# A pad of 224 bytes and one of 192: DMA-transposed tiles moved onto 256-byte boundaries

## Chip, cores and metric

The kernel runs on one core of a Trainium2 chip. The metric is device time in microseconds (us) of one execution of the whole program; lower is better. The profile is of one execution, and its span runs from the first to the last instruction.

## What is computed

The forward pass and all gradients of one block: a layer norm, multi-head attention (32 heads of 16 channels, sequence 2048, width 512) and a gated MLP (hidden width 1792) that multiplies the attention's output. Cut to what matters:

```python
def fwd(A_x, wqkv, wo, w1, b1, w2, b2):          # x: [1, 2048, 512]
    xn = layernorm(A_x)
    q, k, v = split_heads(xn @ wqkv)             # 32 heads, 16 channels each
    p = softmax(q @ k^T * 16 ** -0.5)            # [32, 2048, 2048]
    s = merge_heads(p @ v) @ wo
    h = gelu(layernorm(xn) @ w1 + b1)
    g = silu(h @ w2 + b2)
    return A_x + s * g
# outputs: fwd(...) and the gradients of all seven inputs for a given grad_out, all bf16
```

## The kernel before

**Stages.** `phase_pre` (to about 276 us) does the layer norms, the projections and the MLP forward, and writes per-head-pair operands to DRAM (`NAT_s`, `NATQq_s`, `NATQd_s`). `attention_core` (276 to 2524 us) does the attention forward and backward, with the instruction order as the code writes it. `phase3` (the rest) does the remaining gradients. Instructions of the two outer stages are ordered by the tile framework.

**The attention stage.** It goes over 16 pairs of heads and 4 chunks of 512 queries, 64 blocks of 16 steps; a step `g` takes one block of 128 keys. In a step:

- PE makes the scores `s` (line 648) and, for both heads, `d` (line 662, dP minus its row term); ACT writes `et` = exp(`s`) (line 676); DVE writes `gts` = `d` x `et` (line 697).
- PE adds `et` and `gts` into the sums `X` over keys (lines 729, 732, 744).
- For the gradients of K and V the same arrays are needed with queries on the partitions. `gts` is transposed by DMA into `gk` (line 710), one DMA for two steps: 128 partitions x 4096 bytes, 512 KB. Of `exp(s)`, the query blocks 1 and 3 are transposed by DMA from `et` into `ek` (line 716), two DMAs of 256 KB for four steps; blocks 0 and 2 are computed again by PE and ACT as `t` and `e` (lines 634, 684). PE adds `e`, `ek` and `gk` into `Z` (lines 807, 813) one block of 16 steps later, with a further lag of 3 steps.
- Once per pair of heads `NAT`, `NATQq`, `NATQd` are loaded, GpSimd lays them out in `KVPad` and `QDPad`, and two DMA transposes of 512 KB make `KVT` and `QDT` (lines 594, 602).

All DMA transposes, 512 + 512 + 16 + 16 = 1056, are issued on SyncE's queue in program order. Each is cut in tiles of 16 partitions x 128 elements, so that it reads rows of 128 x 2 = 256 bytes of one partition.

**Where tiles lie.** Tiles of a pool get consecutive addresses within a partition, each rounded up to 32 bytes. `persist` comes first and holds the two identities, `eps_t`, `rstd1` and `rstd2`, and everything after follows from its size. In `attention_core`, the pool `opnd` holds the operands (`KVT0` to `acc`), then come `et` (3 buffers), `gts` (4), `gk` (5), `ek` (10), `e` (5) and small tiles. Sizes from `acc` to `ek` are multiples of 256 bytes, so all buffers of one name have one offset from a 256-byte boundary; all blocks that a transpose reads within a tile start at multiples of 256 bytes from the tile's start.

Of the kernel before, what the change touches and what calls it, by code (L numbers as in the profile page):

```python
# [26 lines left out]
def make_identity(nc, ap):  # L27
    nc.gpsimd.memset(ap, 0.0)
    nc.gpsimd.affine_select(out=ap, in_=ap, compare_op=ALU.not_equal, fill=1.0, base=0,
                            pattern=[[-1, ap.shape[1]]], channel_multiplier=1)  # L30
# [512 lines left out]
def attention_core(ctx, tc, NAT_s, NATQ_s, Oall, dQall, dKVT_out, ident_f32, npairs=16, nqc=4):  # L543
# [4 lines left out]
    opnd = sb("opnd", 1)  # L548
# [27 lines left out]
    Lc = opnd.tile([128, 32], bf16, name="Lc")  # L576
    nc.gpsimd.memset(Lc[:], 0.0)
    nc.gpsimd.memset(Lc[:, 17:18], 1.0)
    acc = opnd.tile([64, S], f32, name="acc")

    def load_ops(p):
# [284 lines left out]
def full_kernel(ctx, tc, A_x, A_wqkv, A_wo, B_x, B_w1, B_b1, B_w2, B_b2, grad_out,  # L866
                out_0, out_1, out_2, out_3, out_4, out_5, out_6, out_7, dbg=None, phases=("01", "15", "att", "3")):
    nc = tc.nc
    dbg = dbg or {}
    k = K()  # L870
    persist = ctx.enter_context(tc.tile_pool(name="persist", bufs=1))
    k.ident_bf = persist.tile([128, 128], bf16, name="ident_bf")
    make_identity(nc, k.ident_bf[:])
    k.ident_f = persist.tile([128, 128], f32, name="ident_f")
    make_identity(nc, k.ident_f[:])
    k.eps_t = persist.tile([128, 1], f32, name="eps_t")
    nc.vector.memset(k.eps_t[:], EPS)
    k.rstd1 = persist.tile([128, NT], f32, name="rstd1")
    k.rstd2 = persist.tile([128, NT], f32, name="rstd2")

    def scratch(name, shape, dt=bf16):
        if name in dbg:
            return dbg[name]
        return tc.dram_tile(list(shape), dt, name=name)
    k.XN_s = scratch("XN_s", [S, D])
    k.Y_s = scratch("Y_s", [S, D])
    k.DSO_s = scratch("DSO_s", [S, D])
    k.H1T_s = scratch("H1T_s", [F, S])
    k.HG_s = scratch("HG_s", [S, F])
    k.DH1_s = scratch("DH1_s", [S, F])  # L890
    k.NAT_s = scratch("NAT_s", [NPAIR, 128, NT, 2 * NATW])
    k.NATQq_s = scratch("NATQq_s", [NPAIR, 128, NT, 34])
    k.NATQd_s = scratch("NATQd_s", [NPAIR, 128, NT, 32])
    k.GB_s = scratch("GB_s", [S, 2, D])
    k.dKVT_s = scratch("dKVT_s", [H * 32, S])

    if "01" in phases or "15" in phases:
        phase_pre(ctx, tc, k, A_x, A_wqkv, A_wo, B_w1, B_b1, B_w2, B_b2, grad_out, dbg)
    with ExitStack() as cO:
        pO = cO.enter_context(tc.tile_pool(name="persistO", bufs=1))  # L900
        k.Oall = pO.tile([128, NT, D], bf16, name="Oall")
        k.dQall = pO.tile([128, NT, D], bf16, name="dQall")
        if "att" in phases:
            with ExitStack() as cB:
                with tc.manual_schedule():
                    attention_core(cB, tc, k.NAT_s, (k.NATQq_s, k.NATQd_s), k.Oall, k.dQall, k.dKVT_s, k.ident_f)
        if "3" in phases:
            phase3(ctx, tc, k, A_x, A_wqkv, A_wo, B_w1, B_w2, grad_out, out_0, out_1, out_2, out_3, out_4, out_5, out_6, out_7, dbg)


@with_exitstack
def kernel(
    ctx: ExitStack,
    tc: tile.TileContext,
    A_x: bass.AP,
    A_wqkv: bass.AP,
    A_wo: bass.AP,
    B_x: bass.AP,
    B_w1: bass.AP,
    B_b1: bass.AP,  # L920
    B_w2: bass.AP,
    B_b2: bass.AP,
    grad_out: bass.AP,
    out_0: bass.AP,
    out_1: bass.AP,
    out_2: bass.AP,
    out_3: bass.AP,
    out_4: bass.AP,
    out_5: bass.AP,
    out_6: bass.AP,  # L930
    out_7: bass.AP,
):
    full_kernel(ctx, tc, A_x, A_wqkv, A_wo, B_x, B_w1, B_b1, B_w2, B_b2, grad_out,
                out_0, out_1, out_2, out_3, out_4, out_5, out_6, out_7)
# [30 lines left out]
```

## Time and profile before

| | |
|---|---|
| median of 2 runs | 3130.07 us (3129.59 to 3130.55) |
| the profiled execution | 3131.9 us, span 3130.1 us |
| busy in the span | PE 81%, DVE 65%, ACT 56%, GpSimd 20% |
| DMA traffic | 543.46 MB, mean 174 GB/s |
| DMA packets | 1831694, of which 1754785 under 512 bytes |
| SyncE's DMA queue (q1) | 486.70 MB, 85.3% of 16 engines' span |

A share of DMA is the time that the packets took, summed and divided by 16 engines and the time; packets of one engine can overlap, so that it can pass 1. PE, DVE, ACT, POOL and SP are the tensor, vector, scalar, GpSimd and sync engines; PEld is PE's weight load. In the views "x <- y" in a wait means that x waited until y ended; a row of a table by windows gives the stretch from:to in us, its length, the busy time of each engine, the granted PE clock, the DMA share and GB/s. For a DMA, "to landing" is from the start of its issue to its completion.

### The profile page before, as it was taken

What the parts mean: (1) busy time and instruction counts of PE and PEld (TensorE: products, weight loads), DVE (VectorE), ACT (ScalarE), POOL (GpSimd) and SP (SyncE); (2) the same over time, 40 slices, a digit from 0 to 9 for tenths busy, and PEclk for the clock granted to TensorE, in tenths of its full rate; (3) what the DMA queues carried; (4) which work ended last, traced back from release to release, by engine and by line L of the source; (5) the groups of instructions that cost most, each with busy time, mean ns of one, the idle gap of its engine ahead of it and who ended that gap; (6) DMA issues with size and microseconds to landing.
All of it is one profiled execution on the core that took longest, in us unless ns stands there. A gap on an engine that the chain in (4) does not pass through costs nothing. (4 is left out here: it accounts for less than half of the span.)

```text
span 3130.1 us, 49097 instructions
## 1 busy us (share of the span) xinstructions
PE 2535.6 (81%) x18944; PEld 791.9 (25%) x18944; DVE 2021.1 (65%) x3382; ACT 1755.6 (56%) x1973; POOL 621.0 (20%) x1023
## 2 busy tenths in 40 slices
PE   4786888888888888888888888888888876674977
PEld 2331222222222222222222222222222223332343
DVE  5764676766767676776767676676767745882034
ACT  2443676766667666666767666676767734441020
POOL 1333110111011110111011110101111024882015
PEclk8997898989989898888989899898989987887989
DMA  5435999999999999999999999999999983324531
GB/s 175 114 125 129 196 194 195 196 196 192 196 193 194 194 194 194 191 196 194 193 198 195 193 193 193 195 194 194 189 195 197 190 226 111 105 89 134 137 123 41
DMA packets 1831694, 543.46 MB, mean 174 GB/s; under 512 B 1754785, under 2 KB 1815586, under 8 KB 1831458
## 3 DMA queue, kind: packets, MB, share of 16 engines
q1 hardware_dynamic: 1758066, 486.70, 85.3%
q10 hardware_dynamic: 73392, 53.62, 5.6%
q8 instruction: 148, 2.42, 0.3%
q14 instruction: 88, 0.72, 0.1%
HBM read 65.41 MB, written 55.32 MB: 39 GB/s over the span
## 5 line engine op out<-in xcount | busy, mean ns | idle before, releaser
L697 DVE TENSOR_TENSOR gts<-d,et 128x512 bf16<-128x512 f32 x2048 | 1304.8, 683 | 630.8 <-DMA gk<-gts 274.2
L676 ACT ACTIVATE et<-s 128x1024 bf16<-128x1024 f32 x1024 | 1016.4, 1025 | 189.3 <-DMA ek<-et 82.3
L684 ACT ACTIVATE e<-t 128x1024 bf16<-128x1024 f32 x512 | 523.5, 1023 | 570.6 <-PE t L634 559.2
L662 PE MATMUL d<-QDT,KVT 32*128 32x512 bf16 x2048 | 617.6, 415 | 264.5 <-DVE gts L697 262.0
L648 PE MATMUL s<-QDT,KVT 32*128 32x512 bf16 x2048 | 430.8, 417 | 43.8 <-ACT et L676 29.1
L729 PE MATMUL X<-et,Lc 128*32 128x512 bf16 x2048 | 441.7, 428 | 12.5 <-DVE xs L750 12.3
L732 PE MATMUL X<-et,NAT 128*32 128x512 bf16 x2048 | 439.8, 427 | 0.0
L744 PE MATMUL X<-gts,NAT 128*17 128x512 bf16 x2048 | 437.6, 423 | 0.0
L813 PE MATMUL Z<-gk,W 128*32 128x512 bf16 x2048 | 436.6, 420 | 0.0
L777 POOL TENSOR_TENSOR W<-NATQd,rL 128x128 bf16<-128x128 bf16 x64 | 25.7, 401 | 1560.9 <-DVE rL L772 1560.9
L807 PE MATMUL Z<-e,W 128*32 128x512 bf16 x1024 | 221.6, 426 | 10.6 <-ACT e L684 7.3
L634 PE MATMUL t<-KVT,QDT 32*128 32x512 bf16 x1024 | 219.1, 425 | 0.0
L807 PE MATMUL Z<-ek,W 128*32 128x512 bf16 x1024 | 218.3, 423 | 0.0
L744 PEld LDWEIGHTS <-NAT 128*17 128x17 bf16 x2048 | 93.2, 88 | 488.9 <-issue 488.9
L648 PEld LDWEIGHTS <-KVT 32*128 32x128 bf16 x2048 | 102.4, 92 | 430.6 <-issue 430.0
L662 PEld LDWEIGHTS <-KVT 32*128 32x128 bf16 x2048 | 134.4, 92 | 253.7 <-issue 237.4
L729 PEld LDWEIGHTS <-Lc 128*32 128x32 bf16 x2048 | 105.3, 94 | 198.5 <-issue 198.5
L820 DVE TENSOR_TENSOR acc<-Z,acc 64x512 f32<-64x512 f32 x192 | 129.2, 673 | 21.1 <-PE Z L813 21.1
L807 PEld LDWEIGHTS <-W 128*32 128x32 bf16 x2048 | 121.5, 94 | 55.1 <-issue 48.3
L732 PEld LDWEIGHTS <-NAT 128*32 128x32 bf16 x2048 | 105.2, 100 | 63.0 <-issue 20.7
L813 PEld LDWEIGHTS <-W 128*32 128x32 bf16 x2048 | 106.8, 99 | 10.6 <-issue 4.8
L634 PEld LDWEIGHTS <-QDT 32*128 32x128 bf16 x1024 | 48.8, 92 | 234.7 <-issue 234.7
(200 smaller groups left out, 2611.6 us busy)
## 6 DMA issues: line engine op xcount, KB each, us to landing
gk<-gts SPq DMA_TRANSPOSE x512, 4.6
ek<-et SPq DMA_TRANSPOSE x512, 3.7
HG_s<-hg SPq DMA_DIRECT2D x16, 448.0 KB, 3.1
DH_s<-dh ACTq DMA_DIRECT2D x16, 448.0 KB, 2.5
NAT<-NAT_s SPq DMA_DIRECT2D x16, 264.0 KB, 3.0
GB_s<-gB ACTq DMA_DIRECT2D x16, 256.0 KB, 2.0
dKVT_s<-ob SPq DMA_DIRECT2D x16, 256.0 KB, 3.6
dhc<-DH_s ACTq DMA_DIRECT2D x2, 2048.0 KB, 13.9
```

What stands on the lines that cost most here:

```text
L634: nc.tensor.matmul(t[:, hj, :], lhsT=op["QDT"][r:r + 32, q0:q0 + 128], rhs=op["KVT"][r:r + 32, kc * 512:(kc + 1) * 512], start=True, stop= ...
L648: nc.tensor.matmul(s[:, hj, :], lhsT=op["KVT"][r:r + 32, kb * 128:(kb + 1) * 128], rhs=op["QDT"][r:r + 32, qc * 512:(qc + 1) * 512], start ...
L662: nc.tensor.matmul(d[:], lhsT=op["KVT"][r:r + 32, kb * 128:(kb + 1) * 128], rhs=op["QDT"][r:r + 32, qc * 512:(qc + 1) * 512], start=True, ...
L676: nc.scalar.activation(out=et[:, :, kb % 4, :, :].rearrange("k b h q -> k h b q"), in_=st_s.pop(g)[:].rearrange("k h (b q) -> k h b q", b= ...
L684: nc.scalar.activation(out=e[:], in_=st_t.pop(g)[:], func=ACT.Exp)
L697: nc.vector.tensor_tensor(out=gts[:, kb % 2, hj, :].rearrange("k (b q) -> k b q", b=4), in0=ds[hj][:].rearrange("k (b q) -> k b q", b=4), ...
L729: nc.tensor.matmul(X[64 + 32 * hj:96 + 32 * hj, :], lhsT=Lc[:], rhs=et[:, :, kb % 4, hj, :], start=(kb == 0), stop=False, skip_group_check ...
L732: nc.tensor.matmul(X[32 * hj:32 * hj + 32, :], lhsT=NATt[:, kb, hj, 1:33], rhs=et[:, :, kb % 4, hj, :], start=(kb == 0), stop=(kb == 15), ...
L744: nc.tensor.matmul(X[64 + 32 * hj:64 + 32 * hj + 17, :], lhsT=NATt[:, kb, hj, 0:17], rhs=gts[:, kb % 2, hj, :], start=False, stop=(kb == 1 ...
L807: nc.tensor.matmul(Z[32 * hj:32 * hj + 32, :], lhsT=blk[j]["W1"][:, qb, hj, :], rhs=ev[:, hj], start=(qb == 0), stop=False, tile_position= ...
L813: nc.tensor.matmul(Z[32 * hj:32 * hj + 32, :], lhsT=blk[j]["W2"][:, qb, hj, :], rhs=gv[:, :, :, hj, qb, :], start=False, stop=(qb == 3), t ...
L820: nc.vector.tensor_tensor(out=av, in0=Z[0:64, :], in1=av, op=ALU.add)
```

## The change

Two tiles are allocated that nothing reads or writes: 224 bytes at the end of `persist` and 192 bytes in `opnd` ahead of `acc`.

```diff
@@ attention_core
     Lc = opnd.tile([128, 32], bf16, name="Lc")
     nc.gpsimd.memset(Lc[:], 0.0)
     nc.gpsimd.memset(Lc[:, 17:18], 1.0)
+    opnd.tile([128, 192], mybir.dt.uint8, name="pad_to_256b")
     acc = opnd.tile([64, S], f32, name="acc")
@@ full_kernel
     k.rstd1 = persist.tile([128, NT], f32, name="rstd1")
     k.rstd2 = persist.tile([128, NT], f32, name="rstd2")
+    persist.tile([128, 224], mybir.dt.uint8, name="pad_to_256")
```

Every engine has the same instructions in the same order with the same waits as before; only addresses differ. The start of the tiles in a partition, as bytes past a 256-byte boundary:

| tile | role in a transpose | before | after |
|---|---|---|---|
| `KVPad`, `QDPad` | read | 32 | 0 |
| `gts` (4 buffers), `et` (3) | read | 96 | 0 |
| `gk` (5), `ek` (10) | written | 96 | 0 |
| `KVT0`, `QDT0` | written | 32 | 0 |
| `KVT1`, `QDT1` | written | 160 | 128 |
| `acc`, `e`, `xs`, `xt`, `W1`, `W2`, `ob` | none | 96 | 0 |
| `Oall`, `dQall`, `xnT`, `yT`, `dsoT`, and the weights loaded in `phase_pre` | none | 32 | 0 |
| `dmT`, `oT`, `dQT`, `xn_all`, `Rkv` and most of `phase3` | none | 64 | 32 |
| `xn`, `y`, `xt4`, `h1row`, `dso`, `hgc`, `dhc` | none | 192 | 160 |
| `h1T`, `xr`, `hg`, `gp`, `dh1` | none | 128 | 96 |

## Prediction

> **What bounds the kernel now.** First the page's totals and its 40 slices, to see which resource is full, and where.
>
> ```profile
> span 3130.1 us, 49097 instructions
> ...
> PE 2535.6 (81%) x18944; PEld 791.9 (25%) x18944; DVE 2021.1 (65%) x3382; ACT 1755.6 (56%) x1973; POOL 621.0 (20%) x1023
> ...
> PE   4786888888888888888888888888888876674977
> ...
> DMA  5435999999999999999999999999999983324531
> GB/s 175 114 125 129 196 194 195 196 196 192 196 193 194 194 194 194 191 196 194 193 198 195 193 193 193 195 194 194 189 195 197 190 226 111 105 89 134 137 123 41
> ...
> q1 hardware_dynamic: 1758066, 486.70, 85.3%
> ```
>
> From the fifth slice to the 32nd the DMA digit is 9, while PE stands at 8. No compute engine is full there. The next view cuts the span at the first transpose (276 us) and after the last one (2524 us).
>
> ```profile
> core 0: us, PE busy (x) PEld busy (x) DVE busy (x) ACT busy (x) POOL busy (x), PEclk, DMA share, GB/s
> 0.00:276.00 276.00, 182.07 (x912) 85.67 (x912) 164.89 (x340) 101.97 (x177) 91.94 (x98) 0.91 0.44 135
> 276.00:2524.00 2248.00, 1925.88 (x15582) 492.77 (x15583) 1555.32 (x2621) 1484.72 (x1532) 267.19 (x698) 0.89 1.11 193
> 2524.00:3130.10 606.10, 427.63 (x2450) 213.42 (x2449) 300.91 (x421) 168.95 (x264) 261.88 (x227) 0.87 0.39 119
> ```
>
> The attention stage is 2248.0 us, 72% of the span. PE is busy for 1925.88/2248 = 86% of it, DVE 69%, ACT 66%. The DMA share of 1.11 (over 1 because packets of one engine overlap) says that the transfers hardly ever stop. They move 193 GB/s x 2248 us = 434 MB, of which the transposes are 512 x 512 KB + 512 x 256 KB + 32 x 512 KB = 419 MB. Whether this stream holds the engines up is read from the waits.
>
> ```profile
> ACT e L684 <- PE t L634: 559.2, 403, 5.7
> ...
> DVE gts L697 <- DMA gk<-gts: 274.2, 132, 4.8
> PE d L662 <- DVE gts L697: 262.0, 558, 4.1
> ...
> ACT et L676 <- DMA ek<-et: 82.3, 74, 2.7
> ```
>
> DVE waits 274.2 us for a transpose to give a `gts` buffer back, ACT 82.3 us for an `et` buffer; PE's largest wait, 262.0 us, is for the DVE multiply that waits there. So the transposes are a real limit: a change of their speed would be seen in the end.
>
> **The change, part by part.** The two pads are allocations that no instruction uses; the instructions, their order and their waits are the same on every engine. The sum has three terms, all of them addresses.
>
> *Term 1, rows read.* The transposes read 512 x 2048 + 512 x 1024 + 32 x 2048 = 1,638,400 rows of 256 bytes, 102,400 on each of the 16 DMA engines. Before, each `gts` or `et` row begins 96 bytes past a boundary (160 bytes before the next one, 96 after), each `KVPad` or `QDPad` row 32 past (224 and 32). After, each lies between two boundaries. No row of this trace shows an aligned transpose, so I compare rates where nothing else, or the least, is in the way.
>
> ```profile
> 278.20:279.60 1.40, 0.00 (x0) 0.00 (x0) 0.00 (x0) 0.00 (x0) 0.37 (x2) 0.50 1.22 213
> 280.20:282.20 2.00, 0.00 (x0) 0.00 (x0) 0.00 (x0) 0.00 (x0) 0.00 (x0) 0.50 1.16 217
> 290.40:292.60 2.20, 2.20 (x16) 0.23 (x10) 1.99 (x4) 1.72 (x2) 0.00 (x0) 0.50 1.12 214
> 1006.00:1007.00 1.00, 0.74 (x10) 0.29 (x10) 0.52 (x1) 1.00 (x2) 0.14 (x1) 1.00 1.15 217
> 1013.40:1014.60 1.20, 1.20 (x18) 0.33 (x14) 0.95 (x4) 1.20 (x2) 0.83 (x3) 0.76 0.05 5
> 1015.00:1016.40 1.40, 1.18 (x8) 0.30 (x7) 1.40 (x3) 1.24 (x2) 1.27 (x4) 1.00 1.27 287
> 2612.20:2613.40 1.20, 0.00 (x0) 0.00 (x0) 0.12 (x1) 1.18 (x4) 0.73 (x1) 0.50 1.25 284
> ```
>
> The last number is GB/s. Row 1 is the first KVT transpose and row 2 the first QDT transpose (source 32 past the boundary), row 3 the first `gk` transpose alone (96 past), row 4 the middle of the stage. All give 213 to 217: neither where the row is cut nor the compute beside it matters. 216 GB/s over 16 engines is 256/13.5 = 19.0 ns a row. Row 5 is a stretch in which the stream stands, and row 6 what follows: the same `gk` transposes, 96 past the boundary, at 287 GB/s, 14.3 ns a row. Row 7 is a plain load of 256-byte rows out of DRAM (`h1T`): 284. So a misaligned row can be read as fast as a plain transfer moves a row of this size; what holds the stream at 216 in the steady state is something else, which an address need not touch. My reading, argued and not shown, is the supply of descriptors, since the fast stretch follows one in which a supply can pile up.
>
> Bounds: nothing at one end; at the other, every row goes at 287. Then 102,400 x (19.0 - 14.3) ns = 481 us of DMA time go, but PE's 1925.88 us remain, so at most 2248 - 1926 = 322 us of the stage. I take 0, as the rows nearest to the case, 1 to 4, show no effect of the offset. A small gain could stay in the fast stretches alone: if alignment saved a row there the same 4.7 ns again, some 106 of them (below) x 1.4 us x 4.7/14.3 = 49 us.
>
> ```profile
> q8 instruction: 148, 2.42, 0.3%
> ...
> q8 instruction: 1, 0.02, 4.0%
> ```
>
> The 106 is an estimate: the page's 148 packets of the instruction queue, 2.42 MB/148 = 16 KB each, times 2248/3130. The second line is the same queue from 1011.5 to 1013 us: one such packet lies just ahead of the stall in row 5, and I count one stall for each.
>
> The Trainium skill's "DMA: Bandwidth & Descriptors", section "How a descriptor splits into AXI transactions", speaks for a gain: a read must start on a 256-byte boundary, and the bytes fetched ahead of a descriptor's start cost beats of 32 bytes. By that account a `gts` row costs 8 + 3 = 11 beats, a `KVPad` row 8 + 1 = 9, an aligned row 8. The trace does not bear out the step from 11 to 9 (214 against 213 to 217); the step to 8, which also makes one transaction of two, no run shows. By the rule alone the stream would rise to 216 x 11/8 = 297 GB/s.
>
> *Term 2, rows written.* `gk`, `ek`, `KVT0` and `QDT0` go to 0 past a boundary; `KVT1` and `QDT1` go from 160 to 128, so for these 16 of 1056 transposes the change does only half of what it says. KVT0 (row 1) is written at 32, `gk` (row 3) at 96, at one rate: 0.
>
> *Term 3, everything else.* The first pad shifts all tiles of the other stages by 224: those at 64 past a boundary go to 32, those at 192 to 160. I price it by operations that stand at both offsets now.
>
> ```profile
> L56 ACT COPY xnT<-tp_ps x16: 585/585/592, 33.0 to 42.2; 128x512 bf16<-128x512 bf16 x16
> ...
> L56 ACT COPY dmT<-tp_ps x16: 585/585/586, 2544.3 to 2567.3; 128x512 bf16<-128x512 bf16 x16
> ...
> L56 ACT COPY dQT<-tp_ps x8: 592/592/592, 3014.6 to 3033.3; 128x512 bf16<-128x512 bf16 x8
> ...
> DMA to landing us min/median/max: 8.5/8.5/8.5
> ```
>
> `xnT` lies at 32, `dmT` and `dQT` at 64: 585, 585 and 592 ns. The last line is of the two `wqkv` loads, one into a tile at 32, one at 64: both 8.5 us. I take 0; the 7 ns between equal offsets, 1.2% of 276 + 606 us, bounds it at 11 us either way.
>
> Sum: 0. The profiled execution took 3131.9 us (span 3130.1 and 1.8 around it), 1.8 above the median of the runs, 3130.07, so the forecast in runs is **3130**. Its own range is 3130 - 49 to 3130 + 11, rounded out to 3080 to 3150. A measurement of this kernel tells about 2% (63 us) from no change.
>
> **The rivals.**
>
> *Faster: the cut costs.* Reading a row in two pieces is what keeps the steady state at 216 GB/s, wherever the cut lies; row 6 then would be rows already read while the stream stood. Aligned rows run near 287, DMA needs 434/287 = 1512 us and PE becomes the bound. For it: rows 1 to 4 are all cut rows, so they cannot exclude it. Against it: row 6 lasts 1.4 us, 287 x 1.4 = 402 KB, a quarter more than 216 would move, some 6 KB for each engine to have held back. Half of the 322 us is my price, since PE now has idle of its own beside the DMA's (its waits for DVE): 161 us, 2970.
>
> *Slower: equal starts collide.* Every row and every destination in the stage now begins on the same boundary, and the 16 engines' accesses could meet more often. What decides it is the steady rate: 2% of the kernel is lost when it falls from 216 below 434/(2009 + 63) = 209, as 434/216 = 2009 us of the stage are streaming.
>
> ```profile
> 277.60:282.40 4.80, 0.00 (x0) 0.00 (x0) 0.00 (x0) 0.00 (x0) 0.76 (x2) 0.50 1.15 205
> ```
>
> At 205, the rate of the two first transposes with the change-over between them, streaming takes 434/205 = 2117 us, 108 more: 3240. Against it: source and destination of a `gk` transpose have equal offsets now too (96 and 96), and shift together.
>
> *It does not do what it says:* 16 transposes of 1056, above; no time of its own.
>
> **How the numbers follow.** No effect 0.70, because offsets 32 and 96 give one rate and misaligned rows reach the rate of a plain transfer. Faster 0.22, because no aligned transpose has been seen and the stream is a limit. Slower 0.08, for want of a place where it shows. The prediction is the likeliest, 3130. Its own range holds about 0.70; down to 2950, past the faster rival's 2970, adds somewhat over half of 0.22. The range is 2950 to 3150, with under 0.2 left out: the larger gains and the slower case. Chances: faster by over 2% 0.22, within 2% 0.70, slower 0.08.
>
> **What would show it.** In the profile after: if term 1 is nil, the `gk` transpose alone, near 290 us, still moves 213 to 217 GB/s, the stage stays near 193, and DVE's wait for `gk` near 274 us. If the faster rival holds, that lone transpose runs well over 230 GB/s, the median landing falls from these values, and PE's share of the stage rises over 90%.
>
> ```profile
> gk<-gts SPq DMA_TRANSPOSE x512, 4.6
> ek<-et SPq DMA_TRANSPOSE x512, 3.7
> ```
>
> If the slower one holds, it falls under 209. Term 3 is wrong if the first 276 us or the last 606 us change by over 11 us. What makes the whole forecast wrong is a steady rate that hangs on a row being cut at all.

## The result, and the profile after

| | before | after |
|---|---|---|
| median | 3130.07 us | 2839.99 us (2839.52 to 2840.47) |
| ratio, 95% interval | | 0.9073 (0.9034 to 0.9112) |
| span of the profiled execution | 3130.1 us | 2837.7 us |
| mean granted PE clock | 0.889 | 0.949 |

The change is 9.3% faster, well below the range of the forecast. From the pad in `opnd` on, line numbers of the kernel are one higher than before (line 697 is now 698). First the page after: totals, clock and transfers in 40 slices, and the landing of the transposes.

```profile
span 2837.7 us, 49038 instructions
...
PE 2383.5 (84%) x18885; PEld 779.8 (27%) x18944; DVE 2013.4 (71%) x3382; ACT 1739.4 (61%) x1973; POOL 620.1 (22%) x1023
...
PEclk8898899999999999999999999999999978887989
DMA  5434999999999999999999999999999853326331
GB/s 178 110 131 121 213 224 225 219 221 226 220 225 225 221 218 222 229 218 227 220 224 219 231 219 221 224 224 226 217 225 225 214 168 98 103 82 162 110 131 41
...
q1 hardware_dynamic: 1758066, 486.70, 84.1%
...
gk<-gts SPq DMA_TRANSPOSE x512, 4.1
ek<-et SPq DMA_TRANSPOSE x512, 3.1
```

Packets and bytes are the same to the last digit (the PE count is 59 lower because the trace lacks some matmul records; the kernel has the same 18944). In the attention stage the transfers run at 213 to 231 GB/s a slice instead of 189 to 198, and a `gk` transpose lands 4.1 us after its issue instead of 4.6. By stage (columns as in the prediction: stretch, length, busy time of PE, PEld, DVE, ACT, POOL, PE clock, DMA share, GB/s):

```profile
0.00:274.20 274.20, 181.42 (x895) 85.90 (x912) 165.25 (x340) 102.00 (x177) 91.91 (x98) 0.91 0.43 136
274.20:2236.00 1961.80, 1782.71 (x15592) 479.51 (x15592) 1546.80 (x2621) 1470.79 (x1535) 267.12 (x698) 0.98 1.13 222
2236.00:2837.70 601.70, 419.40 (x2400) 214.41 (x2440) 301.38 (x421) 166.56 (x262) 261.03 (x227) 0.86 0.39 119
```

All but 6 us of the gain is the attention stage: 2248.0 to 1961.8, 286 us. In it PE's idle time fell from 2248.0 - 1925.9 = 322 to 1961.8 - 1782.7 = 179 us, 143 less, and PE's busy time fell by another 143 us, with the same matmuls at a granted clock of 0.98 instead of 0.89. The same three transposes that the prediction looked at, KVT, QDT and the first `gk`, each in its middle:

```profile
276.00:277.40 1.40, 0.00 (x0) 0.00 (x0) 0.00 (x0) 0.00 (x0) 0.69 (x2) 0.50 1.27 285
278.10:279.50 1.40, 0.00 (x0) 0.00 (x0) 0.00 (x0) 0.00 (x0) 0.00 (x0) 0.50 1.27 290
287.60:289.20 1.60, 1.40 (x14) 0.18 (x10) 1.60 (x3) 1.34 (x2) 0.00 (x0) 0.82 1.27 289
...
1005.60:1007.80 2.20, 1.98 (x18) 0.51 (x16) 1.96 (x4) 1.47 (x3) 0.00 (x0) 1.00 1.25 280
```

They ran at 213, 217 and 214 GB/s before; the last row is the middle of the stage, where the kernel before had 217. 289 GB/s is a mean of 14.2 ns for a 256-byte row on one of 16 engines, against 19.0: 4.8 ns less. The waits of the compute engines follow:

```profile
ACT e L685 <- PE t L635: 453.9, 496, 5.0
...
PE d L663 <- DVE gts L698: 148.5, 525, 3.7
...
DVE gts L698 <- DMA gk<-gts: 58.3, 30, 4.5
...
ACT et L677 <- DMA ek<-et: 6.2, 8, 1.4
```

DVE's wait for a free `gts` buffer went from 274.2 to 58.3 us, PE's wait for DVE from 262.0 to 148.5, and ACT's wait for an `et` buffer from 82.3 to 6.2.

### The profile page after: what moved, and what is told of

It is laid out like the page before. It is cut to its first block, busy times and chain, and to the rows that moved or that the text cites. A ratio compares the mean times of both kernels' runs of the same rounds, so it can differ in the third digit from the quotient of the medians.

```text
span 2837.7 us, 49038 instructions
## 1 busy us (share of the span) xinstructions
PE 2383.5 (84%) x18885; PEld 779.8 (27%) x18944; DVE 2013.4 (71%) x3382; ACT 1739.4 (61%) x1973; POOL 620.1 (22%) x1023
## 5 line engine op out<-in xcount | busy, mean ns | idle before, releaser
L677 ACT ACTIVATE et<-s 128x1024 bf16<-128x1024 f32 x1024 | 1000.5, 1024 | 29.8 <-PE d L663 11.5
L663 PE MATMUL d<-QDT,KVT 32*128 32x512 bf16 x2048 | 598.1, 383 | 150.2 <-DVE gts L698 148.5
L649 PE MATMUL s<-QDT,KVT 32*128 32x512 bf16 x2048 | 402.8, 390 | 18.2 <-DMA QDT<-QDPad 13.2
L730 PE MATMUL X<-et,Lc 128*32 128x512 bf16 x2048 | 404.3, 391 | 14.3 <-DVE xs L751 14.3
L733 PE MATMUL X<-et,NAT 128*32 128x512 bf16 x2048 | 404.7, 392 | 0.0
L745 PE MATMUL X<-gts,NAT 128*17 128x512 bf16 x2048 | 402.4, 389 | 0.0
L814 PE MATMUL Z<-gk,W 128*32 128x512 bf16 x2048 | 401.0, 385 | 0.0
L808 PE MATMUL Z<-e,W 128*32 128x512 bf16 x1024 | 202.5, 389 | 4.7 <-DVE acc L821 2.3
L808 PE MATMUL Z<-ek,W 128*32 128x512 bf16 x1024 | 204.4, 395 | 0.0
L635 PE MATMUL t<-KVT,QDT 32*128 32x512 bf16 x1024 | 201.5, 390 | 0.0
```

Of the source, the lines that this page charges most:

```text
L635: nc.tensor.matmul(t[:, hj, :], lhsT=op["QDT"][r:r + 32, q0:q0 + 128], rhs=op["KVT"][r:r + 32, kc * 512:(kc + 1) * 512], start=True, stop= ...
L649: nc.tensor.matmul(s[:, hj, :], lhsT=op["KVT"][r:r + 32, kb * 128:(kb + 1) * 128], rhs=op["QDT"][r:r + 32, qc * 512:(qc + 1) * 512], start ...
L663: nc.tensor.matmul(d[:], lhsT=op["KVT"][r:r + 32, kb * 128:(kb + 1) * 128], rhs=op["QDT"][r:r + 32, qc * 512:(qc + 1) * 512], start=True, ...
L677: nc.scalar.activation(out=et[:, :, kb % 4, :, :].rearrange("k b h q -> k h b q"), in_=st_s.pop(g)[:].rearrange("k h (b q) -> k h b q", b= ...
L730: nc.tensor.matmul(X[64 + 32 * hj:96 + 32 * hj, :], lhsT=Lc[:], rhs=et[:, :, kb % 4, hj, :], start=(kb == 0), stop=False, skip_group_check ...
L733: nc.tensor.matmul(X[32 * hj:32 * hj + 32, :], lhsT=NATt[:, kb, hj, 1:33], rhs=et[:, :, kb % 4, hj, :], start=(kb == 0), stop=(kb == 15), ...
```

## The experiments

Theory R, formed from this result: a source row that lies across a 256-byte boundary costs the DMA extra time, and where the destination begins does not matter. Each median below is compared with runs of the kernel before on the same chip.

**Source or destination.** Both kernels take the changed kernel and move some tiles by further pads; offsets are bytes past a 256-byte boundary. The edits shown are against the changed kernel. A row that lies across a boundary is called cut, and a transpose that runs with no other beside it a lone one.

```diff
 # e1_dst_off: gk, ek at 96; everything else as changed
+    sb("pad_gk_p", 1).tile([128, 96], mybir.dt.uint8, name="pad_gk")
     gbp = sb("gbp", 5)
     ekp = sb("ekp", 10)
+    sb("pad_e_p", 1).tile([128, 160], mybir.dt.uint8, name="pad_e")
 # e2_src_off: et, gts (and acc) at 96; everything else as changed
-    opnd.tile([128, 192], mybir.dt.uint8, name="pad_to_256b")
+    opnd.tile([128, 288], mybir.dt.uint8, name="pad_acc")
+    sb("pad_gk_p", 1).tile([128, 160], mybir.dt.uint8, name="pad_gk")
     gbp = sb("gbp", 5)
```

> Sources (gts, et, KVPad, QDPad) at 0 past a 256-byte boundary, destinations gk and ek back at 96, all else as in the changed kernel. Theory R (a cut source row costs): as the changed kernel, 2840 us, granted clock 0.95, a lone gk transpose near 289 GB/s. Rival W (where the 32-byte writes begin decides): back to 3130 us, lone gk near 216 GB/s, clock 0.89.

> Sources gts and et back at 96 past a boundary, KVPad and QDPad and all destinations at 0. Theory R: 3130 us, the lone gk transpose at 216 GB/s, but the lone KVT and QDT transposes at the stage's start near 289 GB/s within the same run. Rival W: 2840 us and 289 GB/s for both.

e1 took 2846.1 us, ratio 0.9101 (0.9080 to 0.9123); e2 took 3107.5 us, 0.9928 (0.9912 to 0.9945). e2 is 0.7% faster than before, not equal to it: `KVPad` and `QDPad`, 4% of the bytes, are aligned in it, which may be why. Windows of e2 in its lone KVT, QDT and `gk` transposes:

```profile
274.20:275.80 1.60, 0.00 (x0) 0.00 (x0) 0.00 (x0) 0.00 (x0) 0.76 (x2) 0.50 1.23 280
276.30:278.00 1.70, 0.00 (x0) 0.00 (x0) 0.00 (x0) 0.00 (x0) 0.00 (x0) 0.50 1.23 276
286.00:288.20 2.20, 2.02 (x19) 0.32 (x14) 2.17 (x4) 1.82 (x2) 0.00 (x0) 0.83 1.13 213
```

Within one run, aligned sources (`KVPad`, `QDPad`) go at 276 to 280 and cut ones (`gts`) at 213. In e1, with the destination at 96, the lone `gk` goes as in the changed kernel:

```profile
289.20:290.80 1.60, 1.60 (x10) 0.11 (x4) 1.39 (x3) 1.12 (x2) 0.00 (x0) 0.50 1.27 289
```

The source decides; the rival W is out for the one other destination that was tried, 96.

**Which boundary, and what a cut costs.** The same pads with other sizes: in e3 `gts` and `et` at 128 and `KVPad`, `QDPad` at 64, in e4 at 224 and 192, destinations at 0 in both.

```diff
 # e3_src_64_128 (e4_src_192_224: 192, 224, 32)
+    opnd.tile([128, 64], mybir.dt.uint8, name="pad_src")
     KVPad = opnd.tile([128, 16, 4, 32], bf16, name="KVPad")
-    opnd.tile([128, 192], mybir.dt.uint8, name="pad_to_256b")
+    opnd.tile([128, 256], mybir.dt.uint8, name="pad_acc")
+    sb("pad_gk_p", 1).tile([128, 128], mybir.dt.uint8, name="pad_gk")
     gbp = sb("gbp", 5)
```

> Sources gts and et at 128, KVPad and QDPad at 64 past a boundary, destinations at 0. Theory R with the boundary at 256 bytes: both kinds are cut, 3130 us, 213 to 217 GB/s for lone KVT, QDT and gk. Rival G (a granule of 64 bytes, before at 32 and 96 off it): 2840 us, 289 GB/s for both kinds.

> Sources gts and et at 224, KVPad and QDPad at 192 past a boundary, destinations at 0. Theory R, a fixed price for a cut row: 3130 us and 213 to 217 GB/s for both. Rival B (price by the bytes fetched ahead of the row's start, so that a row at 224 is dearer than at 96 and at 32): slower than before; in proportion to 15 beats at 224, 14 at 192 and 11 at 96, the lone gk transpose falls to 216 x 11/15 = 158 GB/s, the lone KVT to 170, and the kernel rises well over 3400 us.

e3 took 3122.0 us, 0.9975 (0.9964 to 0.9986); e4 3125.7 us, 0.9987 (0.9977 to 0.9998). Both are within 0.3% of the kernel before. The lone KVT, QDT and `gk` of e3 (64, 64 and 128), then of e4 (192, 192 and 224):

```profile
274.80:276.80 2.00, 0.00 (x0) 0.00 (x0) 0.00 (x0) 0.00 (x0) 0.61 (x2) 0.50 1.12 205
277.20:279.20 2.00, 0.00 (x0) 0.00 (x0) 0.00 (x0) 0.00 (x0) 0.00 (x0) 0.50 1.13 213
287.30:289.50 2.20, 2.20 (x16) 0.23 (x10) 1.99 (x4) 1.72 (x2) 0.00 (x0) 0.50 1.14 213
```

```profile
277.50:279.60 2.10, 0.00 (x0) 0.00 (x0) 0.00 (x0) 0.00 (x0) 0.71 (x2) 0.50 1.14 205
280.00:282.00 2.00, 0.00 (x0) 0.00 (x0) 0.00 (x0) 0.00 (x0) 0.00 (x0) 0.50 1.16 214
290.10:292.30 2.20, 2.15 (x19) 0.32 (x14) 2.05 (x4) 1.78 (x2) 0.00 (x0) 0.77 1.16 213
```

With the offsets of before, 32 and 96, that makes six offsets, all at 205 to 217; the two at 205 are KVT, expected at 213 to 217, and QDT with the same offsets has 213 and 214. The mean price of a cut row is the same wherever the cut lies, and alignment to 64 or 128 bytes gives nothing. The Trainium skill's "DMA: Bandwidth & Descriptors", section "How a descriptor splits into AXI transactions", had the boundary right; its count of beats (11 at 96, 15 at 224, 8 aligned) does not set the price here. Whether its second transaction does is not shown: these runs show that the cut costs, not by what mechanism.

**One kind aligned.** `gts` at 0, `et` at 96, by 288 bytes ahead of `acc` and 160 between the pools `etp` and `gtp`.

```diff
-    opnd.tile([128, 192], mybir.dt.uint8, name="pad_to_256b")
+    opnd.tile([128, 288], mybir.dt.uint8, name="pad_acc")
     etp = sb("etp", 3)
+    sb("pad_g_p", 1).tile([128, 160], mybir.dt.uint8, name="pad_g")
     gtp = sb("gtp", 4)
```

> Sources gts (and KVPad, QDPad) at 0 past a boundary, et left at 96, destinations at 0. Theory R by rows: the gk transposes are 268 of 419 MB (64%), so about 0.64 of the changed kernel's gain, 2900 to 2990 us; gk near 289 GB/s alone, ek transposes at 216. Rival: the two kinds wait for each other in one queue, so that the slower kind sets the pace: above 3050 us.

The kernel took 2878.8 us, 0.9199 (0.9185 to 0.9212), faster than the range: 250 of the 290 us, 86% of the gain, with 68% of the bytes aligned (`gts`, `KVPad` and `QDPad`). In e2, 4% of the bytes brought 22 us, 8%. So sharing the gain out by bytes came out too low both times, and the rival, that the slower kind sets the pace, is out.

```profile
gk<-gts SPq DMA_TRANSPOSE x512, 4.1
ek<-et SPq DMA_TRANSPOSE x512, 3.5
```

`gk` lands as in the changed kernel, `ek` still needs 3.5 us against 3.1.

**Only the inner tiles moved.** Both pads inside `opnd`, none in `persist`.

```diff
-    persist.tile([128, 224], mybir.dt.uint8, name="pad_to_256")
+    opnd.tile([128, 224], mybir.dt.uint8, name="pad_ops")      # ahead of KVT0
```

> Both pads inside the attention stage's pool (224 bytes ahead of KVT0, 192 ahead of acc), none in persist: the stage's tiles stand as in the changed kernel, the tiles of the two outer stages as before. Theory R (all of the gain is the cut source rows): 2840 us, stages of 274, 1962 and 602 us. Rival T (the outer stages' shift by 224 has a price of its own): outer stages differ from the changed kernel's by over 5 us.

The kernel took 2840.9 us, 0.9082 (0.9069 to 0.9096), the changed kernel's time. With the outer tiles back at their old offsets, those stages take what they took with the shift, within 3 us:

```profile
0.00:275.50 275.50, 180.07 (x895) 85.36 (x912) 164.55 (x340) 101.90 (x177) 91.87 (x98) 0.91 0.44 135
275.50:2238.40 1962.90, 1789.42 (x15578) 478.93 (x15578) 1547.69 (x2621) 1469.29 (x1532) 267.10 (x698) 0.97 1.13 221
2238.40:2842.70 604.30, 417.85 (x2414) 214.58 (x2454) 302.17 (x421) 168.93 (x264) 261.33 (x227) 0.87 0.39 119
```

**How much the queue has to carry.** Five kernels change how many of the 16 units of exp(`s`) per block go by DMA; the rest is computed again by PE and ACT. They ask whether the stream limits the kernel before (theory L), and whether it still limits the changed one.

```diff
-    dma_units = tuple((kc, qb) for kc in range(4) for qb in (1, 3))
+    dma_units = tuple((kc, qb) for kc in range(4) for qb in (1,))        # e10 (cut rows), e12 (aligned)
+    ... for qb in ((1, 3) if kc % 2 == 0 else (1,)))                     # e11 (aligned)
+    ... for qb in ((1, 2, 3) if kc % 2 == 0 else (1, 3)))                # e6 (aligned), ekp 13
+    ... for qb in (1, 2, 3))   # e7 (aligned): one transpose for all three, ekp 5, ep 2
```

> The kernel before, rows cut as there, with 4 instead of 8 of 16 units of exp(s) transposed by DMA: 67 MB less through the queue, 4 more t matmul pairs and e activations per block. Theory L (the transposes' stream limits the kernel before): 367 MB at 216 GB/s are 1700 us, the stage falls though PE and ACT do more, PE's clock rises: 2900 to 3000 us. Rival (PE's work limits): 3150 us or more.

> The changed kernel with 4 instead of 8 of 16 units transposed by DMA. Theory L: the stream is no longer the limit (367 MB at 289 GB/s are 1270 us), PE has about 100 us more: 2870 to 2940 us, and the alignment is worth far less than 9% against the same kernel with cut rows (under 3%). Rival: alignment is worth 9% whatever the load on the queue: 2700 us or less.

> The changed kernel with 6 of 16 units transposed by DMA (query block 3 left out for key chunks 1 and 3). If the stream still holds the changed kernel up a little: 2790 to 2835 us; if PE's two extra t pairs cost as much as they spare the queue: 2835 to 2880 us.

> The changed kernel with 10 instead of 8 of 16 query-key units of exp(s) per block transposed by DMA (query block 2 added for key chunks 0 and 2; ekp 13 buffers), so that 2 of 8 t matmul pairs and e activations go. If the transposes now leave room: 33 MB more, 467 MB at 289 GB/s is 1616 us of a stage of 1962, PE sheds about 50 us, 2780 to 2820 us. If the stream is still the limit: 2850 to 2900 us.

> The changed kernel with 12 of 16 units transposed, query blocks 1 to 3 of a key chunk by one DMA of 768 KB instead of two of 256 KB (ekp 5 buffers of three units, ep 2): 4 of 8 t matmul pairs and e activations go. If the transposes leave room: PE sheds about 100 us, 2740 to 2800 us. If the stream is the limit (501 MB at 289 GB/s is 1734 us plus the stalls of over 150 us): 2830 us or more.

| units by DMA | rows cut | rows aligned |
|---|---|---|
| 4 | e10: 2801.1 us, 0.8950 (0.8935 to 0.8965) | e12: 2782.6 us, 0.8892 (0.8879 to 0.8905) |
| 6 | | e11: 2784.1 us, 0.8900 (0.8883 to 0.8918) |
| 8 | before: 3130.1 us | the change: 2840.0 us, 0.9073 (0.9034 to 0.9112) |
| 10 | | e6: 3021.3 us, 0.9661 (0.9630 to 0.9691) |
| 12 | | e7: 2992.2 us, 0.9566 (0.9552 to 0.9581) |

The kernel before gets 10.5% faster with more work on PE and ACT and cut rows left as they are: the stream of transposes was its limit, and theory L holds. With 4 units, alignment is worth 0.7% instead of 9.3%. The sizes were mostly missed: e10, e12 and e11 came out faster than their ranges, and e6 slower than both of its own. The stages of e10 and e12, then e6 and e7:

```profile
277.40:2194.40 1917.00, 1786.18 (x16073) 515.74 (x16073) 1566.36 (x2620) 1672.10 (x1784) 266.51 (x697) 0.99 1.11 192
```

```profile
275.30:2175.70 1900.40, 1776.20 (x16061) 513.95 (x16061) 1567.11 (x2620) 1671.34 (x1784) 265.20 (x694) 1.00 0.96 193
```

```profile
274.50:2411.30 2136.80, 1847.98 (x15328) 473.52 (x15329) 1551.41 (x2621) 1362.90 (x1405) 267.06 (x698) 0.92 1.10 219
273.30:2383.70 2110.40, 1807.50 (x15082) 465.41 (x15083) 1556.27 (x2622) 1248.78 (x1279) 267.61 (x699) 0.91 1.16 238
```

Both 4-unit kernels have PE at 93% of the stage. e11 and e12 beat both the kernel before and the changed one: 11.0 and 11.1% below before, 2% below the change. As they give PE and ACT more to do and the queue less, the stream still holds the changed kernel up. Its queue shows why: SyncE issues one transpose right behind the other (start and duration of the issues, in us):

```profile
1005.83 2.65 SPq L717 DMA_TRANSPOSE ek<-et  x2
1008.58 3.58 SPq L711 DMA_TRANSPOSE gk<-gts  x2
1012.25 2.68 SPq L717 DMA_TRANSPOSE ek<-et  x2
1015.03 5.29 SPq L711 DMA_TRANSPOSE gk<-gts  x2
1020.41 2.61 SPq L717 DMA_TRANSPOSE ek<-et  x2
```

Summed over the stage, these issues take 92% of its time in the changed kernel, 94% in the one before, 93 and 94% in e6 and e7, 90% in e10, 84% in e11 and 70% in e12. Alignment made each transpose shorter, but the queue stayed nearly full.

**The clock.** The changed kernel with 3 `gts` buffers instead of 4 makes DVE wait for `gk` without touching an address's alignment.

```diff
-    gtp = sb("gtp", 4)
+    gtp = sb("gtp", 3)
```

> The changed kernel with 3 gts buffers instead of 4; rows stay aligned. Theory C (the granted PE clock rose because PE was left waiting less, not because of addresses): DVE and so PE wait more for gk, the clock falls below the changed kernel's 0.949, towards 0.90 to 0.93, PE's busy time in the stage rises from 1783 us by 40 us or more at the same matmul count, and the kernel takes 2950 to 3100 us while the lone gk rate stays at 289 GB/s. Rival: the clock follows the addresses, and stays at 0.949 with PE's busy time at 1783 us.

The kernel took 2880.6 us, 0.9208 (0.9189 to 0.9226), less than the 2950 us expected. The direction is that of theory C: the stage's PE busy time rose to 1801 us, 18 more where 40 were expected, and its clock fell from 0.98 to 0.97. But e5, which runs like the changed kernel, also shows 0.97, and 1789 us, so this run alone hardly shows anything of the clock.

```profile
274.30:2265.00 1990.70, 1800.62 (x15572) 477.86 (x15572) 1547.79 (x2621) 1471.41 (x1533) 266.13 (x697) 0.97 1.11 218
```

The larger contrast is e6, above: aligned rows, yet a stage clock of 0.92, PE at 1848 us though it has fewer matmuls, and DVE waiting 210.0 us for `gk`:

```profile
DVE gts L698 <- DMA gk<-gts: 210.0, 110, 5.1
```

And e10 has cut rows and a clock of 0.99. So the clock does not follow the addresses. Over all 14 kernels it goes with PE's idle time in the stage (its length less PE's busy time): 124 to 137 us idle in e12, e10 and e11 at 0.99 to 1.00; 174 to 195 us in e5, the change, e1, e8 and e9 at 0.97 or 0.98; 289 and 303 us in e6 and e7 at 0.92 and 0.91; 322 to 329 us in the kernel before, e3, e2 and e4 at 0.89 or 0.90. That idle time sets the clock is argued from this order, not shown by itself. The Trainium skill's "TensorE: Matmul & The Clock Gate", section "Part 1: The HAM clock gate (the "warmup" mystery)", describes it so: the PE clock is halved after an idle window and released by activity. The traces agree as far as mean clock and idle time go together.

## Why the prediction was wrong

- **What bounds the kernel: right.** The stream of transposes was a limit, and a change of its speed was seen in the end; e10 shows it from the other side.
- **Term 1: this step failed.** From row 6 (the fast stretch after a stall, 287 GB/s) the prediction concluded that a misaligned row can be read as fast as a plain transfer, and that the steady 216 GB/s came from something that an address does not touch. e1 and e2 show the opposite: the source rows' offset alone makes the steady rate of a transpose 213 or 289. The fast stretch is a transient and says nothing of a steady price. The prediction itself named what could undo it, some 6 KB per engine read while the stream stood, and took the size as evidence against (its "a quarter more" is a third: 402 KB against 302). Whether that is what happens in such a stretch no run here tells, and it stays open. The descriptor supply, argued there as the limit, is not needed to explain the rate of 216.
- **Rows 1 to 4: read for more than they held.** That 32 and 96 give one rate was right (and 64, 128, 192, 224 nearly so), but all were cut rows, as the faster rival said. "Cut somewhere else" had been tested by them, "not cut" had not, and the likeliest value was taken from the nearest rows all the same.
- **The faster rival: right mechanism, half the size.** Aligned rows run at 289, near its 287. Its price of 161 us was for PE's idle time alone, and that part came to 143. The other 143 us of the stage's 286 are PE's busy time: the bound "at most 322 us" held 1925.88 us fixed, although the row beside it showed a granted clock of 0.89. That floor moved, and so the gain passed the rival's 2970 and the low end of 2950. PE did not become the only bound either, as e11 shows.
- **Term 2: right.** Destinations at 96 (e1) show no cost clear of the noise: 0.3% between the ratios of e1 and the change, whose intervals overlap. **Term 3: right.** e5 shows no price of the outer tiles' shift: under 3 us a stage, where the prediction's bound was 11.
- **The slower rival** did not show: the lone transposes rose.

## What to carry to other kernels

A DMA transpose that reads 256-byte rows of SBUF should have its source tile on a 256-byte boundary; the destination's offset, tried at 0 and 96, did not matter, and a pad of a few hundred bytes a partition is enough. How much it brings depends on how full the queue is: 9.3% here, 0.7% with half of the `ek` transposes gone. Before an effect is ruled out because two values give the same rate, look whether the untried value differs from both in kind, and do not take a transient after a stall for a steady rate. Where one queue is full, compare relieving it (here 4 transposes fewer per block, 10.5%) with making it faster (9.3%), and do not hold PE's busy time fixed where its clock stands below 1: here 143 us of it went away with the waits.

## What the runs showed of the hardware

- A cut row costs 4.8 ns more than an aligned row's 14.2 in the steady state of these transposes, at six offsets nearly alike (205 to 217 GB/s in the middle of a transpose, against 276 to 290 aligned). This is a mean: in the packet records of the kernel before, 74% of the rows of the lone `gk` transpose (290.4 to 292.6 us) take 18 ns, as 99% of the aligned ones do after, and the rest up to 92 ns (records of one engine overlap, so their mean is above 14.2).
- Cut rows still reach 287 GB/s for some 1.4 us after a stall of the stream, each at 18 ns. A lone `gk` transpose that starts from a quiet queue does not (216 GB/s from 290.4 to 291.4 us), so a rest alone is not enough. That would fit rows fetched ahead by transposes already issued; no run here varied it.
- Half the bytes do not take half of the queue's time. In the changed kernel the issue of an `ek` transpose (256 KB) took 1.30 us in the median and 1.25 at the least, though its bytes at 289 GB/s are 0.91 us; a `gk` (512 KB) took 1.82 us, and its bytes at 289 are 1.81. By an estimate from these medians, two of each move 1.57 MB in 6.24 us, 252 GB/s; the stage's mean of 222 has the stalls of the stream in it too, such as the one in row 5 of the prediction.
- At 10 units the aligned kernel took 181 us more than at 8. At the stage's mean of 222 GB/s the 33.6 MB added are 151 us, the greater part. e7 carries 67 MB more than the change, in 256 instead of 512 `ek` transposes, moves 238 GB/s in the stage and loses 152 us. Fewer and larger transposes may be why, but e7 also has other buffers and less work for PE, and the runs do not separate these.
